# A new table of rank shifts, an earlier first weight chunk, and a last output tile copied out in halves

## The chip, the cores and the metric

The kernel runs on one core of a Trainium2 chip. The metric is device microseconds (us) of one execution, as a median of several runs; lower is better. In the profile PE is TensorE (matmuls), DVE is VectorE, ACT is ScalarE, POOL is GpSimd and SP is SyncE, which here issues the DMAs.

## The reference

Three blocks run one after the other, all in fp32 (B=4, H=8, S=576, D=64; 2304 tokens, d_model 512, d_ff 768 and 2048):

```python
# attention, causal, with a bias from a running sum of s
scores = q @ k.T / sqrt(D)
cum    = cumsum(max(s, 0))
scores = where(causal, -1e9, scores + min(-(cum_i - cum_j), 0))
attn   = softmax(scores)
x      = (attn @ v).reshape(tokens, 512)
# expert block with a maximum
h = max(x @ w1, x @ w2, x @ w3);  x = h @ w_out
# rational block
h = x @ w_in
P = a0 + a1*h + a2*h^2 + a3*h^3;  Q = 1 + |b0|*|h| + |b1|*h^2
out = (P / (Q + 1e-6)) @ w_out2
```

## The kernel before, in words

The 32 heads are worked in 16 pairs, numbered 0 to 15. The work on a pair has these steps, each a function of the kernel:

- load: q and k (raw_k, raw_q) and v come in by DMA; `dm` (L279) is the one line that issues all DMAs, on SP's queue. The first two pairs' q and k are 288 KB each.
- prep and prep_pe: q and k are transposed and split into a high and a low part (L485 on PE, L492, or L500 on DVE), into the tile qkT. The bias rows of the running sum go into the tiles EXT, by DMA out of PT, where the running sum is worked out at the start (L410 to L452).
- scores: PE multiplies qkT and EXT (L548) into PSUM banks; DVE adds the causal mask and takes row maxima (L575, tiles P and PD; the results go to the tile small).
- norm: DVE works out the normalising factors (L601, L602), ACT takes the exponentials, POOL scales P and PD (L592).
- flip: PE turns P and PD by a matmul with an identity (L659, L654), and ACT, DVE or POOL copy the result into PT (L273).
- values: PE multiplies PT with v (L721) into a bank, in two parts per pair: part 0 is 256 columns, part 1 is 320. The high half is copied out by ACT or DVE (L273), and the low half is formed by DVE (L734). The bank is free only after L734.

Every product that needs full fp32 is made of three passes over high and low halves. Of the four pairs of a batch come 288 tokens at a time of x, and the experts (L222, 12 or 9 matmuls of 288 columns for a group) multiply them with w1, w2 and w3, with the maximum on DVE (L855). A weight chunk is loaded raw (raww, 512 KB), decoded by DVE in three instructions which hold one PSUM bank from the first to the third (L763, L766, L768), and then split into high and low (L273, L276). From about 410 us on, only the expert output and the rational block run (L1027 to L1106).

The order of the instructions is not the order of the source. Each function hands steps to a `Plan` (L44): a list of engines that may do it, a rank, what it reads and writes, and how many of the eight PSUM banks it takes and frees. `Plan.issue` (L93) is a list scheduler: it keeps a clock of its own for each engine, takes the step that can start first, and between several ready on one engine takes the one with the lowest rank. A step for which several engines are named is given to one by this same clock. A bank is handed out in the order in which the banks come free by that clock. What comes out is one fixed queue for each engine; on the chip every engine works through its queue in order and waits by semaphores for data and for banks. `MOVES` (L19) is a table that is added to the ranks: a key such as ("values", (2, 1)) shifts the step "values" of pair 2, part 1, by so much.

On SP's queue the first five DMAs are s and the q and k of pairs 0 and 1. Then come the EXT rows (which wait for DVE's L452), and then the rest. A weight chunk's load names the first two EXT DMAs, `e_dma[:2]`, as steps that must be placed ahead of it (`weights`, L806).

The last output block (n = NBLK-1, 384 tokens) has three tiles of 128 rows by 512 columns. After the last matmuls (L1092) tile 0 is copied out of its bank by ACT, tile 1 by DVE, tile 2 by ACT (L1106), and each goes out by a DMA.

Of the kernel before, what the change touches and what calls it, by code (L numbers as in the profile page):

```python
# [16 lines left out]


MOVES = {k: x for kind, moves in {  # L19
    "flip": {(1, 0): 0.65, (1, 3): -1.55, (1, 4): 1.7, (3, 2): 1.05, (3, 3): 1.0, (5, 0): 0.1, (5, 3): -0.15,  # L20
        (8, 0): 0.6, (10, 0): 0.7, (12, 1): 1.35, (13, 0): 1.35, (13, 1): 1.4},
    "load v": {5: -0.35, 6: 0.6},
    "norm": {(4, 1): 0.55, (13, 1): -1.2},
    "prep": {3: 1.0, 4: 1.45, 14: 1.75},
    "regroup": {6: 0.65, 8: 1.15, 9: 1.1, 12: 1.5},
    "scores": {(0, 3): -1.1, (1, 1): 0.3, (1, 3): -0.95, (3, 2): -1.9, (3, 3): -0.4, (4, 0): 0.1, (4, 1): 0.6,
        (4, 2): 0.25, (5, 2): -0.1, (6, 1): -0.55, (7, 0): 0.75, (7, 3): 0.95, (9, 2): 0.55, (10, 3): 0.85,
        (11, 0): 1.1, (13, 3): 1.75, (14, 2): 1.85},
    "spill": {0: 0.7, 3: 1.55, 4: 1.5, 10: 0.6, 14: -1.9, 16: -1.3, 18: -1.1, 20: -1.25},
    "values": {(2, 1): 0.65, 5: 0.6, 6: 1.3, 7: 0.35, 9: 1.05, 10: 2.0, 11: 1.0, 12: 1.65, 13: 2.0, 14: 0.75},  # L30
# [3 lines left out]
}.items() for k, x in ((((kind, *k) if isinstance(k, tuple) else (kind, k)), x) for k, x in moves.items())}  # L34


# [134 lines left out]
def kernel(  # L171
# [20 lines left out]
    nc = tc.nc  # L192
    B, H, S, D = q.shape
    NT, DM = out.shape
# [7 lines left out]
    NBLK = NT // TB  # L202
# [48 lines left out]
    def ve(rank, n, fn, reads=(), writes=(), free=(), cost=None):  # L251
        return plan.add({"dve": cost or c_dve(n)}, rank, fn, reads, writes, (), free)
# [25 lines left out]
    def dm(rank, kb, out, in_, reads=(), writes=(), pre=()):  # L278
        return plan.add({"sp": 0.69 if kb in (64, 80) else 0.5}, rank, lambda: nc.sync.dma_start(  # L279
            out=out() if callable(out) else out, in_=in_() if callable(in_) else in_), reads, writes, kb=kb, pre=pre)  # L280
# [94 lines left out]
        nc.gpsimd.memset(t, 1.0)  # L375
    dm(-9, 74, s_in, s.rearrange("b h s -> (b h) s"), (), ["sc0"])

    def load_qk(pr, rank, pre=()):


        b, h = divmod(2 * pr, H)
        if pr in (0, 1, 2):
            for nm, src in (("k", k), ("q", q)):
                t, key = raw_of(pr, nm)
                dm(rank, 288, t[:, 0:S], src[b, h:h + 2].rearrange("y (p f) d -> (y p) (f d)", p=64),
                   [key], [("raw", pr, nm)], pre)
            return
        for nm, src in (("k", k), ("q", q)):
            t, key = raw_of(pr, nm)
            for y in range(2):  # L390
                x = src[b, h + y].rearrange("(p f) d -> p (f d)", p=32)
                for u in range(2):
                    dm(rank, 143, t[64 * y + 32 * u:64 * y + 32 * u + 32, 0:1120],
                       x[:, 32 * u:32 * u + 1120], [key], [("raw", pr, nm, y, u)], pre)
# [59 lines left out]
    e_dma = []  # L454
# [285 lines left out]
    def cols(w, fc):  # L740

        return w.bitcast(U32).rearrange("(k p) f -> p k f", p=128)[:, :, 256 * fc:256 * fc + 256]
# [4 lines left out]
    def load_raw(rank, dst, src, key, pre=()):  # L747

        def view():
            r = dst() if callable(dst) else dst  # L750
            return r.rearrange("p (k f) t -> p k (f t)", k=src.shape[1]) if len(src.shape) == 3 else r.rearrange("p f t -> p (f t)")

        dm(rank, 512, view, src, (), [key], pre=pre)
# [26 lines left out]
    spill = [x[1:] for x in need if x[1:] not in DIRECT]  # L780
# [25 lines left out]
    def weights():  # L806
        for i in range(3 * KF1):
            fc, m = divmod(i, 3)
            plan.tag = ("w", i)
            rank = m_rank(0, 6 * fc) - 1.6  # L810
            r = raww[i % 2]
            key = w13_key[m, fc] = wkey()

            def new(m=m, fc=fc):
                w13[m, fc] = wslot(f"w13_{fc}_{m}")

            plan.add({"ctl": 0.0}, rank, new, (), [key, "w order"])
            load_raw(rank, r, cols((w1, w2, w3)[m], fc), ("raww", i % 2), e_dma[:2])
            decode(rank, lambda r=r: r, lambda i=i: wx[i % 2], ("raww", i % 2), ("wx", i % 2), True)
            split(rank, lambda i=i: wx[i % 2].bitcast(F32), lambda m=m, fc=fc: w13[m, fc], ("wx", i % 2), key, PR(0 if i < 6 else 9))  # L820
        for i, (kind, x) in enumerate(spill):
            plan.tag = ("spill", i)
            rank = S0 + (S1 - S0) * i / len(spill)
            r = raww[i % 2]
            load_raw(rank - 0.3, r, w2_src(kind, x), ("raww", i % 2))
            decode(rank, lambda r=r: r, lambda i=i: wx[i % 2], ("raww", i % 2), ("wx", i % 2), True)
            dm(rank, 256, w2_dram[i], wx[i % 2].bitcast(F32), [("wx", i % 2)], [("spill", i)])
        plan.tag = None
# [253 lines left out]
    def m2_out(rank, n, fc):  # L1082
        kg = ("g", (n * KF2 + fc) % 4)
        for tt in range(TB // 128):
            if fc == 0:
                acc[n, tt] = Hold()
            hold = acc[n, tt]

            def mms(tt=tt, hold=hold):
                ts = slice(128 * tt, 128 * tt + 128)  # L1090
                for x, (ga, wb) in enumerate(((0, 0), (0, 1), (1, 0))):
                    nc.tensor.matmul(hold.bank, t2[kg][:, ga, ts], w2["o2", fc][:, wb, :],  # L1092
                                     start=(fc == 0 and x == 0), stop=(fc == KF2 - 1 and x == 2))

            pe(rank, 3 * 0.231, mms, [kg, w2_key["o2", fc]], [("acc", n, tt)], take=[hold] if fc == 0 else ())
            if fc == KF2 - 1:
                key, = hkeys(1)
                o = {}

                def new(o=o, tt=tt):  # L1100
                    o[0] = pools["p2"].tile([128, DM], F32, tag="h", bufs=KF1, name=f"o{n}_{tt}")

                plan.add({"ctl": 0.0}, rank, new, ["p2"], [key, "h order"])
                on_v = n == NBLK - 1 and tt == 1
                (ve if on_v else ac)(rank, DM, lambda o=o, hold=hold, on_v=on_v: (
                    nc.vector.tensor_copy(o[0], hold.bank) if on_v else nc.scalar.copy(out=o[0], in_=hold.bank)),  # L1106
                    [("acc", n, tt)], [key], free=[hold])
                r0 = n * TB + 128 * tt
                dm(rank, 256, out[r0:r0 + 128, :], lambda o=o: o[0], [key], [("out", n, tt)])

    for dc in range(KM):
        moe1_out(R0 - 0.5, 0, dc)
# [55 lines left out]
```

## Time and profile before

| | |
|---|---|
| runs shown | 867.02 us median of 3 (866.91 to 868.51) |
| profiled execution | 867.21 us, of which the span is 865.4 |
| PE | busy 855.2 us (99%), 6316 matmuls |
| DVE | busy 678.5 us (78%) |
| ACT | busy 531.9 us (61%) |
| POOL | busy 402.1 us (46%) |
| TensorE clock granted | 1.0 in all of the span |
| HBM | 69.96 MB read, 21.60 MB written, 106 GB/s |

The span is what the profiler saw from the first to the last instruction or transfer; 1.8 us of the execution lie around it. Busy time is the sum over an engine's instructions; an engine that is 99% busy can only become faster by having less work or by losing the 1%. The chain that ended last is 95% PE by the page.

### The profile page before, as it was taken

How to read it: one execution, taken by the hardware profiler on the slowest of the kernel's cores; microseconds unless marked ns; L12 is line 12 of the kernel's file. 1: busy time of each engine (PE TensorE's matmuls, PEld its weight loads, DVE VectorE, ACT ScalarE, POOL GpSimd, SP SyncE). 2: the span in 40 equal slices, each digit the busy share in tenths (PEclk: the TensorE clock that was granted, in tenths of full speed). 3: DMA queues.
4: the chain of work that ended last, by engine and by line, in shares of the span. 5: the costliest groups of instructions: out<-in, count | busy, mean ns of one | idle time of the engine just before them, and what ended most of it. 6: DMA issues, size and time to landing. Idle time of an engine off the chain costs nothing.

```text
span 865.4 us, 17650 instructions
## 1 busy us (share of the span) xinstructions
PE 855.2 (99%) x6316; PEld 797.1 (92%) x6316; DVE 678.5 (78%) x1547; ACT 531.9 (61%) x1193; POOL 402.1 (46%) x549
## 2 busy tenths in 40 slices
PE   8899999999999999999999999999999999999998
PEld 7788999999999999999899999999999999999996
DVE  7999998999998875875993886578568748865785
ACT  6887777766766661226763765476367637654664
POOL 5576786756656440007642543354255325432332
PEclk9999999999999999999999999999999999999999
DMA  5987878878866645853000200020020001000100
GB/s 147 217 211 204 220 188 240 227 221 236 240 191 190 202 165 184 291 146 115 1 1 28 65 1 1 28 65 1 1 74 19 1 28 65 0 2 1 37 1 36
DMA packets 80566, 92.77 MB, mean 107 GB/s; under 512 B 33696, under 2 KB 61856, under 8 KB 80448
## 3 DMA queue, kind: packets, MB, share of 16 engines
q1 hardware_dynamic: 80480, 91.67, 36.8%
q8 instruction: 49, 0.80, 0.4%
q14 instruction: 37, 0.30, 0.1%
HBM read 69.96 MB, written 21.60 MB: 106 GB/s over the span
## 4 chain that ended last, share of the span: by engine, by line
PE 95%; DVE 1%; POOL 1%; DMA 1%; issue 0%; ACT 0%; SPq 0%; POOLq 0%; DVEq 0%
PE bank L222 58%; PE bank L1092 23%; PE bank L548 6%; PE bank L721 5%; PE bank L659 2%; PE bank L654 1%; DMA v<-in_v_dram 0%; DMA EXT<-PT 0%; DVE PD L575 0%; PE bank L485 0%; POOL mask L418 0%; POOL PD L592 0%; POOL qkT L276 0%; ACT PD L583 0%; POOL EXT L413 0%
## 5 line engine op out<-in xcount | busy, mean ns | idle before, releaser
L222 PE MATMUL bank<-x,w 128*128 128x288 f32 x1728 | 238.6, 296 | 0.0
L222 PEld LDWEIGHTS bank<-x,w 128*128 128x128 f32 x1728 | 230.2, 188 | 1.9 <-issue 0.2
L1092 PE MATMUL bank<-ws,g 128*128 128x512 f32 x864 | 215.6, 393 | 0.0
L222 PE MATMUL bank<-x,ws 128*128 128x384 f32 x1008 | 190.2, 336 | 0.0
L1092 PEld LDWEIGHTS bank<-ws,g 128*128 128x128 f32 x864 | 160.9, 188 | 29.5 <-DVE g L1072 0.3
L222 PEld LDWEIGHTS bank<-x,ws 128*128 128x128 f32 x1008 | 178.2, 188 | 7.1
L1048 POOL TENSOR_SCALAR q<-a,cf 128x384 f32<-128x384 f32 x96 | 66.2, 690 | 182.5 <-ACT a L1043 181.3
L1050 POOL TENSOR_TENSOR q<-q,a 128x384 f32<-128x384 f32 x96 | 98.4, 1025 | 8.0
L1065 DVE SCALAR_TENSOR_TENSOR q<-q,cf,bank 128x384 f32<-128x384 f32 x96 | 58.8, 613 | 50.7 <-ACT bank L1063 48.0
L276 POOL TENSOR_TENSOR h<-h 128x384 fp32r<-128x384 f32 x30 | 31.2, 1061 | 136.9 <-ACT h L959 136.9
L1071 ACT CAST g<-t 128x384 fp32r<-128x384 f32 x96 | 49.4, 514 | 49.6 <-DVE t L1069 49.6
L1060 ACT ACTIVATE a<-q,cf 128x384 f32<-128x384 f32 x96 | 59.3, 617 | 31.3 <-POOL q L1050 30.5
L222 PE MATMUL bank<-h,ws 128*128 128x384 f32 x432 | 75.9, 336 | 0.0
L222 PEld LDWEIGHTS bank<-h,ws 128*128 128x128 f32 x432 | 75.0, 188 | 0.5
L1043 ACT ACTIVATE a<-bank 128x384 f32<-128x384 f32 x96 | 47.0, 489 | 41.0 <-PE bank L222 40.5
L1051 DVE TENSOR_TENSOR t<-bank,t 128x384 f32<-128x384 f32 x96 | 52.9, 551 | 21.6 <-ACT t L1045 21.6
L273 POOL COPY PT<-PD 32x576 f32<-32x576 f32 x94 | 62.2, 661 | 14.2 <-DVE PD L634 9.9
L1045 ACT ACTIVATE t<-bank,cf 128x384 f32<-128x384 f32 x96 | 64.0, 666 | 0.0
L1052 DVE SCALAR_TENSOR_TENSOR t<-t,cf,bank 128x384 f32<-128x384 f32 x96 | 58.8, 612 | 2.4
L1069 DVE SCALAR_TENSOR_TENSOR t<-t,cf,bank 128x384 f32<-128x384 f32 x96 | 58.7, 611 | 2.4
L855 DVE TENSOR_TENSOR hs<-bank,hs 128x288 f32<-128x288 f32 x96 | 43.0, 448 | 20.2 <-PE bank L222 19.2
L592 POOL TENSOR_SCALAR PD<-PD,small 128x640 f32<-128x640 f32 (+3 forms) x38 | 27.6, 736 | 63.3 <-DVE small L602 57.6
(115 smaller groups left out, 1370.4 us busy)
## 6 DMA issues: line engine op xcount, KB each, us to landing
raww<-in_moe_w_out_dram SPq DMA_DIRECT2D x22, 512.0 KB, 4.2
raww<-in_moe_w_dram SPq DMA_DIRECT2D x18, 512.0 KB, 4.5
w_dram<-wx SPq DMA_DIRECT2D x36, 256.0 KB, 4.5
ws<-w_dram SPq DMA_DIRECT2D x36, 256.0 KB, 4.5
raw_k<-in_k_dram SPq DMA_DIRECT2D x52, 140.0 KB, 6.4
raw_q<-in_q_dram SPq DMA_DIRECT2D x52, 140.0 KB, 4.3
raww<-in_moe_w_in_dram SPq DMA_DIRECT2D x14, 512.0 KB, 5.2
h_dram<-hs SPq DMA_DIRECT2D x48, 144.0 KB, 3.4
```

What stands on the lines that cost most here:

```text
L222: nc.tensor.matmul(ps, l, r, start=begin and i == 0, stop=end and i == len(seq) - 1)
L273: nc.scalar.copy(out=out, in_=in_) if e == "act" else (nc.vector if e == "dve" else nc.gpsimd).tensor_copy(out, in_)
L548: nc.tensor.matmul(holds[g][y].bank[0:nr, at0:at0 + j1 - j0], l[h, r0:r0 + nr], keys, start=(x == 0), stop=(x == len(ops) - 1))
L1045: ac(rank, 0, lambda: nc.scalar.activation(out=t2[kt], in_=hold.bank[:, 0:TB], func=ACTF.Identity, scale=cf[:, 3:4], bias=cf[:, 2:3]), [(" ...
L1048: po(rank, 0, lambda: nc.gpsimd.tensor_scalar(t2[kq], t2[ka], cf[:, 5:6], cf[:, 4:5], ALU.mult, ALU.add), [ka, "cf4"], [kq], cost=0.75)
L1050: po(rank, 0, lambda: nc.gpsimd.tensor_tensor(t2[kq], t2[kq], t2[ka], ALU.mult), [ka], [kq], cost=0.97)
L1051: ve(rank, TB, lambda: nc.vector.tensor_tensor(t2[kt], hold.bank[:, 0:TB], t2[kt], ALU.mult), [("hp", ci)], [kt])
L1052: ve(rank, 0, lambda: nc.vector.scalar_tensor_tensor(t2[kt], t2[kt], cf[:, 1:2], hold.bank[:, 0:TB], ALU.add, ALU.mult), [("hp", ci), ("h ...
L1060: ac(rank, 0, lambda: nc.scalar.activation(out=t2[a], in_=t2[qq], func=ACTF.Ln, bias=cf[:, 6:7], scale=1.0), [kq, "cf6"], [ka], cost=0.52)
L1065: ve(rank, 0, lambda: nc.vector.scalar_tensor_tensor(t2[qq], t2[qq], cf[:, 6:7], hold.bank[:, 0:TB], ALU.add, ALU.mult), [kr], [kq], cost= ...
L1069: ve(rank, 0, lambda: nc.vector.scalar_tensor_tensor(t2[t], t2[t], cf[:, 0:1], hold.bank[:, 0:TB], ALU.add, ALU.mult), [kr, turn], [kt], f ...
L1092: nc.tensor.matmul(hold.bank, t2[kg][:, ga, ts], w2["o2", fc][:, wb, :], start=(fc == 0 and x == 0), stop=(fc == KF2 - 1 and x == 2))
```

## The change

Four edits. The table of rank shifts has other keys and other values; the load of weight chunk 0 no longer names the EXT DMAs as steps to be placed ahead of it; `load_qk` has got a parameter whose default keeps what it did; and the last output tile is copied out of its bank in two halves, columns 0 to 255 by ACT and 256 to 511 by DVE, with the DMA behind both. The lines of the new file are 1 further down between L378 and L1090 (L548 is L549), and the copies at the end are L1109 and L1112.

```diff
 MOVES = {k: x for kind, moves in {
-    "values": {(2, 1): 0.65, 5: 0.6, 6: 1.3, 7: 0.35, 9: 1.05, 10: 2.0, 11: 1.0, 12: 1.65, 13: 2.0, 14: 0.75},
+    "values": {(2, 1): 1.7, (3, 1): 1.0, 7: 0.95, 8: 1.1, 9: 0.7, 11: 2.0},
...
-    def load_qk(pr, rank, pre=()):
+    def load_qk(pr, rank, pre=(), names="kq"):
...
-            for nm, src in (("k", k), ("q", q)):
+            for nm in names:
+                src = {"k": k, "q": q}[nm]
...
-            load_raw(rank, r, cols((w1, w2, w3)[m], fc), ("raww", i % 2), e_dma[:2])
+            load_raw(rank, r, cols((w1, w2, w3)[m], fc), ("raww", i % 2), e_dma[:2] if i else ())
...
-                (ve if on_v else ac)(rank, DM, lambda o=o, hold=hold, on_v=on_v: (
-                    nc.vector.tensor_copy(o[0], hold.bank) if on_v else nc.scalar.copy(out=o[0], in_=hold.bank)),
+
+                half = DM // 2 if n == NBLK - 1 and tt == 2 else DM
+                (ve if on_v else ac)(rank, half, lambda o=o, hold=hold, on_v=on_v, half=half: (
+                    nc.vector.tensor_copy(o[0], hold.bank) if on_v else nc.scalar.copy(out=o[0][:, 0:half], in_=hold.bank[:, 0:half])),
                     [("acc", n, tt)], [key], free=[hold])
+                if half < DM:
+                    ve(rank, half, lambda o=o, hold=hold, half=half: nc.vector.tensor_copy(o[0][:, half:], hold.bank[:, half:]),
+                       [("acc", n, tt), "h order"], [("o", "end")])
                 r0 = n * TB + 128 * tt
-                dm(rank, 256, out[r0:r0 + 128, :], lambda o=o: o[0], [key], [("out", n, tt)])
+                dm(rank, 256, out[r0:r0 + 128, :], lambda o=o: o[0], [key] + [("o", "end")] * (n == NBLK - 1 and tt == 2), [("out", n, tt)])
```

The number of matmuls is the same. What the edits do to the queues is shown at three places.

The first is the start of the program. SP's queue there, before, from its second DMA on; raww_108 is the buffer of weight chunk 0, and EXT_94 and EXT_95 are the bias rows of pairs 0 and 1.

```order
L279 DMA raw_k<-in_k_dram 128x576
L279 DMA raw_q<-in_q_dram 128x576
L279 DMA raw_k<-in_k_dram 128x576
L279 DMA raw_q<-in_q_dram 128x576
L279 DMA EXT_94<-PT 8x1x1152
L279 DMA EXT_95<-PT 8x1x1152
L279 DMA ext_dram<-PT 32x2880
L279 DMA raw_k<-in_k_dram 128x576
L279 DMA raw_q<-in_q_dram 128x576
```

The same stretch of SP's queue now:

```order
L279 DMA raw_k<-in_k_dram 128x576
L279 DMA raw_q<-in_q_dram 128x576
L279 DMA raw_k<-in_k_dram 128x576
L279 DMA raw_q<-in_q_dram 128x576
L279 DMA raww_108<-in_moe_w_dram 128x4x256
L279 DMA EXT_94<-PT 8x1x1152
L279 DMA EXT_95<-PT 8x1x1152
L279 DMA ext_dram<-PT 32x2880
L279 DMA raw_k<-in_k_dram 128x576
```

The weight chunk, which had been the 24th DMA, stands sixth, in front of the bias rows; pair 2's raw_q has moved behind four loads of v.

The second place is where the values of pair 3 end and the next scores of pair 4 begin. DVE's queue there, before (x3_127 is the x tile that the values fill):

```order
L500 STREAM_TRANSPOSE T_k_93<-raw_k_89 128x18x32
L734 TENSOR_TENSOR x3_127<-bank1_67,x3_127 128x320
L500 STREAM_TRANSPOSE T_q_92<-raw_q_88 128x18x32
L273 COPY PT_100<-bank4_70 128x4x128
L273 COPY PT_100<-bank2_68 128x4x128
```

The same place of DVE's queue now (x3_130 is the x tile of pair 3 there, and raww0_108 is a weight chunk):

```order
L735 TENSOR_TENSOR x2_126<-bank1_67,x2_126 128x256
L764 TENSOR_SCALAR bank3_69<-raww0_108 128x512
L273 CAST x3_130<-bank7_73 128x320
L273 COPY PT_100<-bank0_66 128x3x128
L735 TENSOR_TENSOR x3_130<-bank7_73,x3_130 128x320
L767 SCALAR_TENSOR_TENSOR bank3_69<-raww0_108,bank3_69 128x512
```

The subtraction for pair 3's values of 320 columns frees bank7 now, and bank1 before; it is the 176th entry of DVE's queue, and was the 170th.

PE's queue at the same place, before, from the values of pair 3 to the scores of pair 4 (PD_96 holds scaled scores, qkT0_90 the q and k of pair 4).

```order
L721 MATMUL bank1_67<-PT_100 64x64 x2
L222 MATMUL bank6_72<-x0_124,w13_0_1_129 128x288
...
L659 MATMUL bank7_73<-ident_87,PD_96 128x128 x3
L659 MATMUL bank4_70<-ident_87,PD_96 128x128 x4
L659 MATMUL bank2_68<-ident_87,PD_96 128x128 x4
L222 MATMUL bank5_71<-x3_127,w13_0_0_128 128x288 x3
L222 MATMUL bank6_72<-x3_127,w13_0_1_129 128x288 x3
L548 MATMUL bank1_67<-qkT0_90 128x256
L548 MATMUL bank7_73<-qkT0_90 128x256
```

The same place of PE's queue now:

```order
L722 MATMUL bank7_73<-PT_100 64x64 x2
L660 MATMUL bank0_66<-ident_87,PD_96 128x128 x3
L660 MATMUL bank6_72<-ident_87,PD_96 128x128 x4
L660 MATMUL bank1_67<-ident_87,PD_96 128x128 x4
L549 MATMUL bank0_66<-qkT0_90 64x64
L549 MATMUL bank7_73<-qkT0_90 64x64
```

In both orders the next scores of pair 4 take the bank into which the values of pair 3 went (bank1 before, bank7 now). Before, 15 expert matmuls and the flips stand between the two, now the flips alone.

The third place is the end of the program: the last rows of ACT's queue and then of DVE's, before (o5_0 to o5_2 are the last three output tiles, and what an instruction waits for stands in brackets):

```order
L1071 CAST g2_3_5501<-t2_3_5493 128x384 [waits DVE_49,PE_49]
L1106 COPY o5_0_8826<-bank4_70 128x512 [waits PE_49]
L1106 COPY o5_2_8828<-bank0_66 128x512 [waits PE_49]
L1072 TENSOR_TENSOR g2_3_5501<-t2_3_5493,g2_3_5501 128x384 [waits PE_49,Activation_49]
L1106 COPY o5_1_8827<-bank6_72 128x512 [waits DMAHW4_49,DMAHW3_49,DMAHW5_49,DMAHW2_49,PE_49]
```

The same ends now, ACT's two rows first and then DVE's three:

```order
L1109 COPY o5_0_8826<-bank7_73 128x512 [waits PE_49]
L1109 COPY o5_2_8828<-bank6_72 128x256 [waits DVE_49]
L1073 TENSOR_TENSOR g2_3_5501<-t2_3_5493,g2_3_5501 128x384 [waits PE_49,Activation_49]
L1109 COPY o5_1_8827<-bank3_69 128x512 [waits DMAHW4_49,DMAHW3_49,DMAHW5_49,DMAHW2_49,PE_49]
L1112 COPY o5_2_8828<-bank6_72 128x256 [waits DMAHW7_49,DMAHW6_49,PE_49]
```

ACT's copy of the last tile waits for DVE where it waited for PE; DVE's half stands behind DVE's copy of tile 1.

## Rows read from the trace of the kernel before

**Rows 1.** Busy time by stretch: stretch, length, then busy (instructions) of each engine.
```profile
core 0: us, PE busy (x) PEld busy (x) DVE busy (x) ACT busy (x) POOL busy (x), PEclk, DMA share, GB/s
16.50:73.00 56.50, 53.48 (x606) 45.34 (x602) 55.01 (x174) 47.62 (x145) 32.10 (x46) 1.00 0.84 201
73.00:861.60 788.60, 788.55 (x5475) 739.62 (x5475) 611.96 (x1340) 474.47 (x1026) 360.76 (x478) 1.00 0.33 99
```

**Rows 2.** PE's waits up to 73 us: total us, times, longest.
```profile
PE bank L659 <- POOL PD L592: 1.5, 2, 1.4
PE bank L440 <- POOL ident masks.py:199: 1.5, 1, 1.5
PE bank L485 <- DVE small L575: 1.5, 1, 1.5
PE bank L721 <- ACT PT L273: 0.6, 1, 0.6
PE bank L721 <- DVE PT L273: 0.6, 1, 0.6
PE bank L548 <- DMA EXT<-PT: 0.4, 1, 0.4
```

**Rows 3.** Busy time by stretch, DVE alone.
```profile
0.00:58.30 58.30, 51.95 (x171) 1.00 0.79 193
```

**Rows 4.** DVE's timeline to 16.5 us: start, length, instruction, [idle before it <- releaser].
```profile
11.05 0.49 DVE L575 CUSTOM_DVE_ANT_0 P<-bank,mask 128x320 f32<-128x320 f32 x1 [0.62 <-PE bank L548]
...
16.50 0.62 DVE L575 CUSTOM_DVE_ANT_0 PD<-bank,mask 128x448 f32<-128x448 f32 x1 [1.19 <-PE bank L548]
```

**Rows 5.** DVE's groups, 16.5 to 73 us: count, busy us, mean ns, idle before.
```profile
L763 DVE TENSOR_SCALAR bank<-raww 128x512 uint32<-128x512 uint32 x6 | 4.1, 676 | 0.0
L734 DVE TENSOR_TENSOR x<-bank,x 128x256 fp32r<-128x256 f32 x4 | 1.6, 410 | 0.0
L273 DVE CAST x<-bank 128x320 fp32r<-128x320 f32 x1 | 0.5, 450 | 0.0
```

**Rows 6.** DVE's timeline at the values of pair 3.
```profile
57.82 0.48 DVE L734 TENSOR_TENSOR x<-bank,x 128x320 fp32r<-128x320 f32 x1
58.22 1.23 DVE L500 STREAM_TRANSPOSE T_q<-raw_q 128x576 f32<-128x576 f32 x1
59.30 1.26 DVE L273 COPY PT<-bank 128x512 f32<-128x512 f32 x2
60.49 0.20 DVE L575 CUSTOM_DVE_ANT_0 P<-bank,mask 64x64 f32<-64x64 f32 x1
```

**Rows 7.** PE's timeline at the scores of pair 4.
```profile
57.30 1.42 PE L659 MATMUL bank<-ident,PD 128*128 128x128 f32 x11
58.47 1.04 PE L222 MATMUL bank<-x,w 128*128 128x288 f32 x6
59.44 0.62 PE L548 MATMUL bank<-qkT 64*128 64x256 f32 x6
```

**Rows 8.** The chain that ended last: start, length, piece, matmuls in it.
```profile
155.75 1.78 PE bank L222 x12
...
158.07 1.58 PE bank L222 x12
```

**Rows 9.** SP's timeline, two DMA issues of the first 7 us.
```profile
2.60 0.43 SPq L279 DMA_DIRECT2D raw_q<-in_q_dram  x1
6.72 1.54 SPq L279 DMA_DIRECT2D EXT<-PT  x2
```

**Rows 10.** The chain's piece for the bias rows.
```profile
6.72 3.23 DMA EXT<-PT
```

**Rows 11.** DMA busy by stretch, last two columns: share, GB/s.
```profile
4.00:5.00 1.00, 1.00 (x14) 0.78 (x15) 1.00 (x1) 0.00 (x0) 1.00 (x1) 1.00 1.00 339
6.00:7.00 1.00, 1.00 (x42) 1.00 (x40) 0.94 (x2) 0.59 (x1) 1.00 (x2) 1.00 0.05 18
```

**Rows 12.** Timeline of the end, ACT and DVE.
```profile
860.91 0.69 DVE L1106 COPY o<-bank 128x512 f32<-128x512 f32 x1 [2.86 <-PE bank L1092]
861.59 0.59 ACT L1106 COPY o<-bank 128x512 f32<-128x512 f32 x1 [0.77 <-PE bank L1092]
```

**Rows 13.** ACT's groups over the whole program.
```profile
L273 ACT CAST x<-bank 128x256 fp32r<-128x256 f32 x16 | 5.9, 366 | 2.8 <-PE bank L721 2.8
```

More of the change, by code (lines that the diff above doesn't have):

```diff
@@ L19 @@
 MOVES = {k: x for kind, moves in {
[L20 to L29, printed above, removed]
-    "values": {(2, 1): 0.65, 5: 0.6, 6: 1.3, 7: 0.35, 9: 1.05, 10: 2.0, 11: 1.0, 12: 1.65, 13: 2.0, 14: 0.75},
[3 rows of a table removed]
+    "flip": {(2, 2): 0.15, (2, 3): 0.45, (3, 3): -0.2, (3, 4): -1.15, (5, 0): -1.3, (11, 0): -1.1, (12, 1): 1.95,
+        (14, 0): 0.8},
+    "load v": {2: 0.55, 12: -0.2, 13: 0.25},
+    "norm": {(0, 1): 1.55, (2, 1): -0.45, (14, 1): 0.1, (14, 3): 1.75, (15, 3): 2.0},
+    "prep": {2: 1.6, 3: 0.8},
+    "regroup": {8: 1.8, 9: 1.95, 10: 0.55, 12: 1.6},
+    "scores": {(1, 1): 1.55, (1, 3): -1.45, (4, 0): -0.7, (5, 0): 0.55, (6, 2): 0.8, (7, 1): 1.9, (7, 2): -1.4,
+        (8, 0): -0.9, (9, 1): -0.35, (10, 2): -1.25, (10, 3): -0.55, (12, 1): 1.45, (12, 3): 1.9, (13, 3): -1.15,
+        (14, 1): -1.9, (15, 2): -1.15, (15, 3): 0.7},
+    "spill": {0: 1.95, 1: 1.75, 2: 0.75, 4: 0.55, 6: -1.35, 10: -1.2, 11: -0.25, 14: -1.8, 25: 1.7, 27: -1.1},
+    "values": {(2, 1): 1.7, (3, 1): 1.0, 7: 0.95, 8: 1.1, 9: 0.7, 11: 2.0},
[3 rows of a table added]
 }.items() for k, x in ((((kind, *k) if isinstance(k, tuple) else (kind, k)), x) for k, x in moves.items())}
```

6 rows, old and new, of the table MOVES are left out of this document.

## The prediction

> **What bounds the kernel now.** I read the busy time by stretch first, then PE's waits, then DVE's queue, then the end. From 73 us to the last matmuls PE is busy for 788.55 of 788.60 us [rows 1]: nothing waits there, so a moved instruction can gain nothing there, and costs something only if it makes PE wait. Between 16.5 and 73 us PE lacks 56.50 - 53.48 = 3.02 us, and DVE only 56.50 - 55.01 = 1.49. There DVE is nearly as full as PE, and the two bound the start together. All of PE's waits of more than 0.3 us in the first 73 us are six groups, 6.1 us in all [rows 2]: the first identity (1.5), the bias rows (0.4), a raw_k of pair 2 charged to DVE (1.5, at 12.6 us), and flips and values that wait for P, PD and PT behind DVE, ACT and POOL (2.7). What the change is worth is therefore decided in the first 73 us, in how PE passes between kinds of matmul, and in the copies behind the last matmul. The sum is made against the profiled execution, 867.21 us; the median of the runs shown lies 0.19 below it. By less than 0.2% of it (1.7 us) a measurement of this kernel can't tell a change from none: "same" is 865.3 to 868.75.
>
> **The queues of the first 60 us.** The table moves DVE's work, it hardly removes any. The point to watch is the subtraction that ends pair 3's 320-column values and frees their bank: the next scores of pair 4 take that bank in both orders. Before, it ended at 58.29 (57.82 + 0.48, less rounding) [rows 6], and the scores began at 59.44 [rows 7], so the bank had been free for 1.15 us and PE didn't wait for it. Now I set DVE's work in front of it against that of before. Successive starts give the net prices: a copy of a flipped block 0.59 (two from 59.30 to 60.49), a transpose 1.08 (58.22 to 59.30) [rows 6]; by the same overlap of about 0.08 to a mean, a decode step 0.59 and a high half 0.35 to 0.45 [rows 5].
> No longer in front of it: one high half of q and k (0.68), three flips (0.60, 0.47, 0.47), two weight splits (0.35, 0.41), a decode step (0.59): 3.6 us. New in front of it: five flips and one decode step (6 x 0.59 = 3.5), a weight subtraction (0.60), three high halves of values that were ACT's (3 x 0.45 = 1.35), a q transpose of pair 5 (1.08): 6.6 us. That is +3.0 us of DVE's work ahead of the same instruction.
> Against it: chunk 0 is loaded early, so DVE can decode it in holes in which it stood before. These are 0.62 us at 11 and 1.19 at 16.5 [rows 4]; two decode steps, 1.2 us, fill them. The instruction then ends at 58.3 + 3.0 - 1.2 = 60.1 us.
> PE meanwhile has less in front of those scores: fifteen expert matmuls have gone from the place between values and scores, others have come ahead; counted by durations, it has 1.9 us less to do there, which is 59.44 - 1.94 = 57.5 with the waits it had before. It would stand from 57.5 to 60.1 and some 0.05 for the signal: 2.65 us. What PE lost by a late DVE afterwards, about 0.6 us near 68 and 72, goes, since DVE's work after this point is the less. Net: **+2.0 us**. Nothing later gives it back, for after 73 us PE has no idle time out of which to take it [rows 1].
> The bounds. Upward: if ACT's queue, which also has more in front of pair 2's and 3's values, makes DVE wait, I get +3.0. Downward: DVE has to do 55.2 us of work by that point, and before it had stood 58.30 - 51.95 = 6.35 us by then [rows 3]; of that at least 2.9 are the beginning, when its inputs have not arrived. So it can't be done before 58.1: PE waits 0.6 there, and the 0.6 saved later pays for it: 0.
>
> **The early chunk.** It is issued behind the fourth load of q and k (from 2.60) instead of behind the EXT rows (from 6.72) [rows 9], at about 3.1, and moves 512 KB in front of them. At the 339 GB/s of the first loads that is 512 KB / 339 = 1.5 us; from 6 to 7 us the DMA engines are at 0.05 of their capacity [rows 11]. By that the first loads are done at about 6, so the chunk ends near 7.5, while the EXT rows are issued at 6.72 and landed at 9.95 [rows 10], and their packets start about 8. Cost: between 0 (the hole hides it) and 1.5 (the EXT rows stand behind all of it, and PE's 0.4 on them grows by that). I take 0. No gain by itself: the first experts aren't what PE waits for [rows 2].
>
> **PE's passages.** Twelve expert matmuls behind flips take 1.58, the same twelve behind scores 1.78 [rows 8]: 0.20 for each return from scores or values to the full array. By the two PE queues there were 36 such returns, and there are now 32: 4 x 0.20 = -0.8. Passages between scores and values go from 23 to 23, with the transposes from 29 to 30: +0.1. Together **-0.7 us**, between -1.0 and -0.4 as other neighbours cost a little more or less.
>
> **The last tile.** ACT's copy of the last bank took 0.59 and began with PE's last matmul [rows 12]; DVE was free by then (860.91 + 0.69 = 861.60). Now ACT's half waits for DVE and no longer for PE, and DVE's half waits for PE: the two halves stand one behind the other. 256 columns out of a bank take DVE 0.41 [rows 5] and ACT 0.37 [rows 13]. One behind the other, with some 0.05 between: 0.83 against 0.59, **+0.25 us**. Side by side it would be the longer half, 0.41: -0.2. The Trainium skill, "PSUM — Partial Sum Buffer", in its table of terms under PSUM bank, says that two engines must not access the same bank in the same quadrant at once, reads against reads included; by that rule halves of columns can't be read side by side, and the dependence in the queue is the rule put into practice. No row here shows two engines on a bank at once, and the sum by the rule is the +0.25 that I take from the queue and these rows anyway; without it the term would be -0.2.
>
> The changed `load_qk` issues what it did: 0. POOL's queue has no term of its own: it is busy 32.10 of 56.50 us in the dense stretch [rows 1], and scaled tiles that come late are inside the bounds above.
>
> **Sum:** 867.21 + 2.0 - 0.7 + 0.25 = 868.76; at the median, 0.19 less: 868.6 us.
>
> **The rivals.**
> (a) DVE is relieved: the early decodes free it for the tiles that PE waits for. For it: 2.7 us of PE's waits end on DVE, ACT or POOL behind DVE [rows 2], and 1.2 us of decoding move into its holes. Against it: the +3.0 us in the queue. It holds if the bank for pair 4's scores is free when PE comes. If 1.2 us of those waits and the 0.6 near 70 us go, with -0.7 and +0.25: 867.02 - 2.25 = 864.8, faster.
> (b) The EXT rows stand behind the chunk: one queue of transfers, 512 KB, 1.5 us. PE's first scores come 1.5 later, DVE's masks with them, and as DVE is full until 73 us all of it stays: 868.6 + 1.5 = 870.1, slower. It decides if the chunk's last packet lands after about 8 us. The empty hole at 6 us speaks against it; that the four loads before it keep all DMA engines full at 4 us [rows 11], so that a little delay pushes it into the EXT rows, for it. ACT's bound of +3.0 without any EXT delay gives 869.6, which I count with this case.
> (c) The waits only change their places: the bank is free 0.6 after PE comes, as by the lower bound. 867.02 + 0 - 0.7 + 0.25 = 866.6, same.
>
> **How the numbers follow.** My forecast gets 0.42, its own range 867.9 to 869.4: it straddles the edge of 868.75, and I split it 0.25 same, 0.17 slower. (a) gets 0.22, all faster. (b) gets 0.20, slower. (c) gets 0.16, same. So faster 0.22, same 0.41, slower 0.37. The range takes in (c), (b) and some of (a): 864.9 to 870.8.
>
> **What would show it.** In the changed kernel's profile: PE's waits have one of 2 to 3 us that ends at about 60 us, at L549 on the bank that DVE's L735 frees, and L735 for the 320 columns ends there, not at 58.3; the waits near 68 and 72 us are gone; after 80 us PE still has none. Twelve expert matmuls still take 1.58 or 1.78. At the end ACT's L1109 of 256 columns starts when DVE's L1112 ends, and the last copy ends some 0.8 after the last matmul. The chunk lands before 8 us, and the wait for EXT stays at 0.4. The forecast is wrong if PE's longest wait up to 73 us lies elsewhere, if DVE frees that bank by 58 us, or if PE's idle time grows after 80 us.

## The result, and the profile after

The changed kernel takes 872.64 us (median of 6, 871.49 to 873.38) against 867.70 (median of 6): ratio 1.0051, 95% interval 1.0041 to 1.0062. It is slower by half a per cent, where 868.6 was forecast with "same" as the likeliest outcome, and it lies above the stated range, whose upper end is 870.8. Four of the six runs had a mean granted TensorE clock of 0.996 to 0.998 and took 872.6 to 873.4. The two at 1.00 took 871.5, which is above the range as well, and most runs of before at 1.00 took 866.8 to 868.5, so some 4 us of the 5 are the change at an even clock. The profiled execution is one of these two, 871.49 us, with a span of 869.9 against 865.4.

Busy time by stretch, after; the columns are those of [rows 1]:

```profile
16.50:73.00 56.50, 51.84 (x595) 43.05 (x594) 55.30 (x175) 48.06 (x144) 34.15 (x48) 1.00 0.83 194
73.00:90.00 17.00, 16.13 (x163) 14.41 (x163) 16.66 (x44) 11.98 (x36) 9.86 (x13) 1.00 0.76 206
90.00:865.90 775.90, 775.60 (x5326) 727.93 (x5324) 598.33 (x1301) 463.02 (x990) 346.55 (x459) 1.00 0.31 96
```

PE lacks 4.66 us from 16.5 to 73 us where it lacked 3.02, then 0.87 more up to 90 and 0.3 after that. PE's waits in the changed kernel, whole program, to be read against [rows 2]:

```profile
PE bank L722 <- ACT PT L273: 1.5, 2, 1.1
PE bank L441 <- POOL ident masks.py:199: 1.5, 1, 1.5
PE bank L486 <- DMA raw_k<-in_k_dram: 1.4, 1, 1.4
PE bank L549 <- DMA EXT<-ext_dram: 1.4, 1, 1.4
PE bank L660 <- DVE x L735: 0.5, 1, 0.5
PE bank L222 <- DVE wx L769: 0.5, 1, 0.5
PE bank L660 <- DVE PT L273: 0.5, 1, 0.5
PE bank L660 <- DVE small L576: 0.4, 1, 0.4
PE bank L549 <- DVE PT L273: 0.2, 1, 0.2
PE bank L222 <- DVE hs L856: 0.2, 1, 0.2
PE bank L549 <- DVE x L735: 0.2, 1, 0.2
```

Seven kinds of waits (those of [rows 2] and one of 0.3) have become eleven. PE's idle time over the whole span grew by only 2.5 us (10.2 to 12.7 us). Its busy time grew by 2.0 with the same 6316 matmuls. Much of that is the first matmul behind a wait, which has a longer record (0.41 us for the two EXT matmuls behind the wait at 28 us, 0.31 elsewhere), so that such a wait costs more than its row says. Counted from the start of one matmul to the start of the next, over what the same pair of matmuls takes elsewhere, the last matmul begins 4.39 us later, and that is made of:

| | before | after | |
|---|---|---|---|
| waits up to 16.5 us | 2.2 | 1.6 | -0.6 |
| the first 136 transposes | 4.65 | 5.37 | +0.7 |
| waits from 16.5 to 62 us | 2.8 | 6.3 | +3.5 |
| waits from 62 to 90 us | 0.7 | 1.1 | +0.4 |
| waits behind 90 us | 0 | 0.7 | +0.7 |
| PE's passages between kinds of matmul | | | -0.9 |
| the rest, differences under 0.06 each | | | +0.6 |

The copies behind the last matmul add 0.23.

The growth of 3.5 us up to 62 us isn't spread evenly. Before, PE's longest wait there was for POOL's PD; in the changed kernel a wait of the same length for pair 2's bias rows stands in its place. Before, then the changed kernel:

```profile
32.54 1.09 PE L659 MATMUL bank<-ident,PD 128*128 128x128 f32 x8 [1.36 <-POOL PD L592]
```

```profile
29.59 0.41 PE L549 MATMUL bank<-EXT 64*128 64x320 f32 x2 [1.37 <-DMA EXT<-ext_dram]
```

Up to 46 us the two kernels differ by 0.6 us. The other 2.9 us lie between 46 and 62 us, where PE waited for nothing before; the first of these waits is 0.53 us, at 47.49 us, for DVE's L735.

### The profile page after: what moved, and what is told of

It reads as the page before. It is cut to its first block, busy times and chain, and to the rows that moved or that the text cites. A ratio compares the mean times of both kernels' runs of the same rounds, so it can differ in the third digit from the quotient of the medians.

```text
span 869.9 us, 17667 instructions
## 1 busy us (share of the span) xinstructions
PE 857.2 (99%) x6316; PEld 798.1 (92%) x6316; DVE 683.3 (79%) x1554; ACT 532.4 (61%) x1192; POOL 399.6 (46%) x544
## 4 chain that ended last, share of the span: by engine, by line
PE 90%; DVE 5%; DMA 3%; issue 1%; POOL 1%; SPq 1%; ACT 0%; POOLq 0%; DVEq 0%; ACTq 0%
PE bank L222 56%; PE bank L1093 23%; PE bank L549 5%; PE bank L722 4%; PE bank L660 1%; DMA raw_k<-in_k_dram 1%; DMA raww<-in_moe_w_dram 1%; SPq L279 1%; DVE PD L576 1%; PE bank L655 1%; DMA ws<-w_dram 1%; DVE bank L764 1%; DVE bank L767 0%; DVE P L576 0%; DVE T_q L501 0%
## 5 line engine op out<-in xcount | busy, mean ns | idle before, releaser
L584 ACT ACTIVATE PD<-PD,small 128x640 f32<-128x640 f32 (+3 forms) x64 | 47.8, 749 | 21.1 <-DVE small L576 19.5
```

## The experiments

A part undone through the source lets the planner write a wholly new order. So two kinds of kernels were run: some with one part of the source alone, and some in which the planner's order was written down first and one or a few steps were moved in it, all else staying where it was. In the diffs, `move(a, b)` puts step a in front of step b of that order, `after(a, b)` behind it. Times "at full clock" are those of runs with a mean granted clock of 0.999 or 1.00.

**The parts alone.** The table without the early chunk, and with the last tile copied whole (`e_moves`; the diff is against the kernel before):

```diff
 MOVES = {k: x for kind, moves in {
-    "values": {(2, 1): 0.65, 5: 0.6, ...
+    "values": {(2, 1): 1.7, (3, 1): 1.0, ...
```

> The kernel before with the new table of rank shifts alone; the first weight chunk behind the bias rows and the last tile copied whole, as before. The planner writes a third order, in which pair 2's bias rows again stand late on SP's queue, behind the coefficients. If the table by itself makes the start dense, PE's waits up to 90 us grow by 2 us or more over before (5.7), and the time is 869.5 to 872 against 868. If the loss comes from the early chunk's place in the queues, the table alone gives the time of before or, by the fewer passages of PE, 0.5 less: 867 to 868.

Measured: 887.19 us, ratio 1.0228 (1.0204 to 1.0252), more than three times the loss of all parts together. Its waits behind 90 us, where before has none and the changed kernel 0.2:

```profile
PE bank L721 <- POOL PT L273: 2.3, 1, 2.3
PE bank L222 <- ACT PT L273: 1.9, 2, 1.1
PE bank L659 <- POOL P L592: 1.3, 1, 1.3
PE bank L654 <- DVE hs L855: 1.0, 2, 0.7
...
```

The early chunk with the old table (`e_early`):

```diff
-            load_raw(rank, r, cols((w1, w2, w3)[m], fc), ("raww", i % 2), e_dma[:2])
+            load_raw(rank, r, cols((w1, w2, w3)[m], fc), ("raww", i % 2), e_dma[:2] if i else ())
```

> The kernel before with the first weight chunk allowed in front of the bias rows, and nothing else; the planner writes a fourth order. If the early chunk's place in the queues makes the loss, the time is 870 to 872; if the table makes it, 867 to 869.

Measured: 874.99 us, ratio 1.0078 (1.0059 to 1.0096). Either part alone has a higher median than both together (for the early chunk the two intervals just touch), so their losses can't be added: each makes the planner write another order. That a table of shifts suits only the order that it was made for fits this, but these two runs don't show more.

**The early transfer by itself** (`x_chunk`: the order of before, with this one DMA moved):

```diff
+    move(96, 16)      # load of weight chunk 0, in front of the first bias rows
```

> The kernel before with one DMA moved: weight chunk 0 is loaded in front of the first bias rows, as in the changed kernel; its decoding and everything else stay where they were. If the chunk only shares the DMA engines with the q and k of pairs 0 and 1 (as in the changed kernel, where the first 136 transposes took 5.4 us for 4.6), the transposes take 0.7 us longer, PE's wait for the first bias rows (0.6) goes, and the time is that of before, 867.7 within 0.3. By case (b) of the prediction the bias rows stand behind the chunk and the time grows by 1 to 1.5 us, 868.7 to 869.2.

Measured: 867.70 us, ratio 0.9996 (0.9987 to 1.0006). PE waits 0.2 and 0.4 us for raw_k and raw_q within the first transposes, and no longer for the bias rows. The transfer by itself costs nothing that this shows (at most 0.5 us by the interval); the loss comes with the order that is written around it.

**The late bias rows of pair 2** (`x_ext`: the order of the changed kernel with one DMA moved). In the changed kernel PE waits 1.4 us at 28 us for this load, issued at 24.3 us where it was issued at 19.3:

```diff
+    move(484, 547)    # EXT<-ext_dram of pair 2, in front of pair 3's raw_k
```

> The changed kernel with one DMA moved: the load of pair 2's bias rows (EXT from ext_dram) goes up SP's queue from behind pair 3's raw_q and the coefficients to in front of pair 3's raw_k, about where the kernel before has it. Nothing else moves on any engine. Theory D (DVE's queue sets the pace from about 49 to 78 us, so a wait that PE loses earlier comes back later): PE's wait of 1.4 us for EXT at 28 us goes, PE's waits from 33 to 78 us grow by as much, and the time falls by 0 to 0.4 us, 872.2 to 872.6, ratio to before 1.005 or a little more. Rival E (the late bias rows are a cause of their own): the 1.5 us are gained in full, about 871.1, ratio 1.004.

Measured: 873.69 us, ratio 1.0050 (1.0036 to 1.0064); 871.1 in the one run at full clock, against 871.5, so of the 1.5 us no more than some 0.4 are gained. One run says little here: some runs of before at that clock took 869 us or more. PE's waits from 25 us on begin with:

```profile
PE bank L660 <- ACT P L591: 1.8, 1, 1.8
PE bank L722 <- ACT PT L273: 1.5, 2, 1.1
```

The wait for EXT is gone, and PE waits 1.8 us for the first flips behind it. This profile alone doesn't tell why: its clock had fallen before (last section), and in `l_after` and `y_pk` below, whose clock fell too, the wait for EXT is gone and the same 1.8 and 1.7 us stand in front of the flips though the load is where it was. That what PE lost at 28 us it would else have lost at 31 fits the time at full clock, but is argued.

**DVE relieved** (`x_dve2`, and `x_extdve2` with the DMA moved too):

```diff
+    for x in seq:     # x[0]: step, x[1]: engine
+        if x[0] in (458, 460, 529, 542, 545, 619, 614): x[1] = "act"
+        if x[0] in (108, 129, 136): x[1] = "pool"
```

> The changed kernel with ten steps of the first 75 us taken from DVE and given to other engines at the same places of the order: four flip copies and three high halves of values to ACT (about 3.6 us of DVE's work), three weight subtractions to POOL (about 1.8 us). Theory D: PE's waits between 46 and 78 us, now 4.1 us, shrink by 2 to 3.5 us, and the time falls to 869.1 to 870.6, ratio to before 1.0016 to 1.0034. Rival E: these waits follow from the late bias rows and from DMAs, and the time stays at 872.6, ratio 1.0057. A third case: ACT, busy 40 of 45 us there, becomes what PE waits for, and the time stays or grows; then the waits carry ACT's name.

> Both edits of the two kernels before this one: the earlier load of pair 2's bias rows, and the ten steps taken from DVE. Theory D: once DVE is relieved the wait at 28 us counts as well, so it gains 0.5 to 1.5 us over the kernel with the ten steps alone: 868 to 870. Rival E: 871.1, as with the bias rows alone.

Measured: 872.08 us, ratio 1.0047 (1.0033 to 1.0062), and 873.28, ratio 1.0049 (1.0037 to 1.0062); at full clock 871.4 to 872.1 and 872.0. Theory D's gain isn't there. PE's waits from 30 to 80 us in `x_dve2`:

```profile
PE bank L722 <- ACT PT L273: 2.0, 2, 1.1
PE bank L549 <- DMA EXT<-ext_dram: 1.8, 1, 1.8
PE bank L660 <- ACT PT L273: 0.5, 1, 0.5
PE bank L549 <- ACT PT L273: 0.4, 1, 0.4
...
```

Apart from EXT, which grew by 0.4, and two of 0.2 that aren't shown here, they carry ACT's name now, the third case: work taken off DVE is work on ACT, which holds the next step.

**Less work for DVE and none more for others** (`l_before`, `l_after`: the orders of before and of the changed kernel; of the three decoding instructions the middle one is left out for each of the first eight weight chunks, so that the weights lack bits):

```diff
+    seq[:] = [x for x in seq if x[0] not in range(98, 98 + 7 * 8, 7)]
```

> The kernel before in its own order, with one of the three decoding instructions left out on DVE for each of the first eight weight chunks (the middle one, so the weights lack bits): about 8 x 0.6 = 4.8 us of DVE's work less, most of it before 85 us, and nothing more for any other engine. By the theory that DVE is the second bound of the start, some of PE's 2.8 us of waits from 30 to 43 us and 0.7 us from 67 to 73 go: 0.5 to 2 us faster than before, 866 to 867.5. By the rival that PE's waits there are the delay of a chain from engine to engine, nothing: 868.

> The changed kernel in its own order, with the same eight instructions left out. By the theory that DVE's load is what the new order runs into, its 4.1 us of waits from 46 to 78 us fall to 1 or less, and it comes within 1 us of the other kernel without these instructions: 867 to 869. By the rival that in the new order PE reaches steps just after the steps that they depend on, so that it waits for the way PE to ACT or DVE and back however free these are, 2.5 us or more of the waits stay: 870 to 871.5.

Measured: 867.50 us, ratio 0.9985 (0.9974 to 0.9996), and 871.78, ratio 1.0037 (1.0023 to 1.0050); at full clock 865.9 to 867.1, and 871.0 in the one such run. The old order gains about a microsecond; the new one gains half of one, though two of its waits behind 73 us are gone. The wait of 1.1 us for PT stays:

```profile
PE bank L660 <- ACT P L591: 1.8, 1, 1.8
PE bank L722 <- ACT PT L273: 1.5, 2, 1.1
PE bank L549 <- DVE PT L273: 0.6, 1, 0.6
PE bank L549 <- DVE x L735: 0.2, 1, 0.2
```

**The order around the wait of 1.1 us.** In the changed kernel PE does pair 3's first flips at 55.06 us and has nothing else between them and the values that need them; ACT copies the flips only at 56.27, behind two exponentials:

```profile
55.06 0.63 PE L660 MATMUL bank<-ident,P 128*128 128x128 f32 x4
55.53 0.54 PE L655 MATMUL bank<-ident,P 128*128 128x128 f32 x3
55.90 0.38 PE L660 MATMUL bank<-ident,P 128*128 128x128 f32 x2
57.38 0.34 PE L722 MATMUL bank<-PT 128*64 128x64 f32 x4 [1.09 <-ACT PT L273]
```

```profile
54.95 0.67 ACT L584 ACTIVATE PD<-PD,small 128x448 f32<-128x448 f32 x1 [0.71 <-DVE small L576]
...
55.62 0.65 ACT L584 ACTIVATE PD<-PD,small 128x448 f32<-128x448 f32 x1
...
56.27 1.05 ACT L273 COPY PT<-bank 128x512 f32<-128x512 f32 x3
```

Before, 32 matmuls of pair 4's scores stood between flips and values. In the changed kernel 16 of them stand in front of the flips and 16 behind the values. `y_swap` moves the first 16 back between the two (its expectation speaks of 32), `y_swap_light` with the eight instructions left out as well:

```diff
+    after(730, 607)   # scores of pair 4, behind the flips of pair 3
```

> The changed kernel with one step of PE's queue moved: the 32 matmuls of pair 4's first scores go from in front of pair 3's first flips to behind them, so that they stand between these flips and pair 3's first values, as in the kernel before. Theory L (order and distance: in the new order the values stand directly behind the flips they need, so PE waits for the way over ACT, 1.2 us at 56 us, whatever the engines' load): the wait of 1.2 us in front of the values goes. But the flips' own inputs are ready only at about 55 us, so that PE may wait up to 1 us in front of the flips instead: 870.3 to 871.5 at full clock against 871.5. By theory D nothing changes, since DVE's queue decides when pair 3's scores are scaled: 871.5.

> The same move, and the eight decoding instructions left out as in the kernel with less work for DVE. Theory L: with DVE lighter the flips' inputs are ready earlier, and the 1.2 us which that kernel still lost in front of the values go: 1 to 1.3 us faster than it, about 869.8 to 870 at full clock. If the wait comes back elsewhere: 871.

Measured: 872.95, ratio 1.0051 (1.0038 to 1.0064), at full clock 872.2 or more; and 872.57, ratio 1.0052 (1.0040 to 1.0064). In `y_swap` the wait moved: 1.1 us in front of the flips, charged to DVE's small, and nothing was gained. The flips' inputs were late too. With 16 matmuls of the 32, this isn't a full test of the old place of these scores. `y_pk` takes one step out of the way of the masks that make them, `y_pk_light` with less work besides:

```diff
+    after(794, 583)   # transpose of pair 5's k, behind the masks and factors of pair 3
+    after(862, 794); after(863, 862)   # the two loads into its buffer follow it
```

> The changed kernel with one step of DVE's queue moved: the transpose of pair 5's k (1.1 us, whose data land at 49.0 us) goes from in front of the four masks of pair 3's second scores to behind them and the factors made of them (the two loads that reuse its buffer follow it). Theory H (head of the queue: the masks stand behind a transpose that waits for its transfer, the scaling stands behind the masks, the flips behind the scaling, the values behind the flips): the masks come 1.1 us earlier, PE's waits from 54 to 57 us, now 1.4, fall by 0.5 to 1.1 us, and the time at full clock falls to 870.4 to 871.0. Theory D (only DVE's total work counts): the same work stands in front of pair 4's scores, so PE waits there instead: 871.5.

> The same move in the kernel without the eight decoding instructions. There DVE stood idle in front of that transpose until the transfer landed, so that the lighter queue gained nothing before 57 us. Theory H: now the lighter queue counts, PE's waits between 54 and 62 us, 2.2 in that kernel, fall to 1 or less, and the time at full clock falls from 871 to about 869.7. If they stay, the transfer is not what held the lighter queue.

Measured: 872.54, ratio 1.0049 (1.0033 to 1.0065), at full clock 871.4 and 872.6: nothing. And 870.55, ratio 1.0031 (1.0020 to 1.0043), at full clock 869.6 to 869.9 with one run of 870.6: some 1.2 us under the kernel with the lighter DVE alone, as theory H has it, though the wait of 1.1 us itself stays. That kernel has one run at full clock (871.0), and the intervals of the two ratios overlap, so this step isn't clear of noise. Both moves together:

> The changed kernel with both moves: pair 5's k transposed behind the masks of pair 3's second scores, and pair 4's first scores behind pair 3's first flips. Either alone left 1.2 us of waiting in front of the values or of the flips. If the two waits are one chain (late masks, late flips, then values directly behind them), both moves together break it: PE's waits between 54 and 58 us fall from 1.4 to 0.5 or less and the time at full clock to 870.3 to 870.8 against 871.5. If not, a wait of about 1.2 us stays at one of the two places: 871.4 or more.

> The same two moves without the eight decoding instructions, where the first move alone gave 869.7 at full clock. If order and load together make the waits, this one falls by another 0.7 to 1.2 us, to 868.5 to 869, within 1 to 2.5 us of the old order without these instructions (866.5 at full clock). If the wait only moves, 869.7.

Measured: 873.34, ratio 1.0054 (1.0041 to 1.0067), and 871.75, ratio 1.0035 (1.0021 to 1.0049). The chain isn't broken: in `y_pk_swap` PE waits 1.0 us in front of the flips, now under POOL's name. POOL's scaling of P stands there behind a copy and two subtractions; the profile ends the wait at POOL's next copy, so which of them held PE isn't settled.

**What the early slot is worth.** PE's wait at 12.6 us, in [rows 2] under DVE's name, is for pair 2's raw_k. `z_rawk` gives the slot in front of the bias rows to it, `z_rawkq` to pair 2's q too (order of before), `a_rawkq` does the same in the order of the changed kernel and puts the chunk behind the bias rows:

```diff
+    move(20, 16)      # raw_k of pair 2, in front of the first bias rows
+    move(21, 16)      # raw_q of pair 2 (not in z_rawk)
+    after(96, 22)     # a_rawkq only: weight chunk 0 behind the bias rows
```

> The kernel before with one DMA moved: pair 2's k is loaded in front of the first bias rows, into the slot that the change gave to the weight chunk. It lands near 8 us, long before PE asks for it at 12.6. If the raw_k of pair 2 is what PE waits for there (1.6 us, charged to DVE by the waits), the wait falls to what raw_q of pair 2 and DVE leave of it, and up to 1.6 us are gained: 866 to 867. If DVE sets the pace, PE's gain comes back as a wait near 15 or 31 us: 867.5. Where the granted clock falls behind this wait in some runs (times of 869 instead of 867.5), it stays at 1.00 in all.

> The same with pair 2's q in front of the bias rows too. Both are there when PE asks for them at 12.6 us, but 576 KB take 1.7 us of the DMA engines behind the first loads, to about 7.7 us, and the bias rows begin at 8. If the bias rows aren't delayed: 865.9 to 867 and the granted clock 1.00 in all runs. If they are, PE waits for them near 10 us, up to 1 us longer, and half of the gain is gone.

> The changed kernel with the early slot given to pair 2's k and q, and the weight chunk loaded behind the bias rows. In the kernel before, the same slot for k and q gained about 1.3 us at full clock. If that wait of 1.6 us at 12.6 counts in the new order as well: 870 to 870.5 at full clock, and the granted clock stays at 1.00 in nearly all runs. If the new order's later waits set the pace: 871.5, with the waits behind 28 us longer by as much.

Measured: `z_rawk` 868.67 us, ratio 0.9999 (0.9989 to 1.0008), with 866.0 to 869.9 in single runs; `z_rawkq` 866.78, ratio 0.9982 (0.9972 to 0.9991); `a_rawkq` 877.45, ratio 1.0106 (1.0090 to 1.0123). In `z_rawkq` the matmuls that began at 14.31 begin at 12.80:

```profile
12.59 0.28 PE L548 MATMUL bank<-EXT 64*128 64x256 f32 x2
12.80 1.15 PE L485 MATMUL bank<-ident,raw_k 64*64 64x64 f32 x32
```

Up to 73 us the later waits keep their length and come 1.2 us earlier: DVE, 98% busy there, wasn't the limit. In this profiled run (866.80) part of the gain is lost again by a new wait of 0.5 us for ACT's x behind 200 us; in that of `z_rawk` (865.99) nothing is. In the other runs of `z_rawk` something else must be late: eight of twelve took more than 868 us, some of them at full clock. In `a_rawkq` DVE, then PE, show why the new order can't do without the early chunk:

```profile
16.26 0.69 DVE L764 TENSOR_SCALAR bank<-raww 128x512 uint32<-128x512 uint32 x1 [6.01 <-DMA raww<-in_moe_w_dram]
```

```profile
PE bank L549 <- DVE qkT L493: 5.0, 1, 5.0
```

The first decoding step stands tenth among DVE's instructions, in front of the last high and low parts of q and k; when its chunk is late, everything behind it is.

**A version below both** (`z_best`): `z_rawkq`, with POOL's scaling of pair 1's PD in front of a copy and a subtraction:

```diff
+    after(557, 456); after(559, 557)
```

> The kernel before with pair 2's k and q in front of the bias rows and, on POOL, the scaling of pair 1's PD tiles (1.4 us) moved in front of the 1.4 us subtraction and the copy for pair 3's q and k, behind which PE waited for it at 31 us. If nothing else holds the flips there, PE's wait of 1.4 us goes: 1.0 to 1.4 us under the kernel with k and q alone, 864.5 to 865.5 at full clock and below both kernels. If the subtraction that is now later holds the scores of pair 3 at 35 us, the wait moves there: 866.

Measured: 866.14 us, ratio 0.9980 (0.9968 to 0.9992), no clear step beyond `z_rawkq`: POOL now stands idle 1.87 us for ACT's PT in front of that scaling, and PE's wait there is 1.0 us instead of 1.3.

## Why the prediction was wrong

- **DVE's queue at pair 4's scores: right in place and time.** L735 for 320 columns was to end at 60.1 us; it ended at 60.69. DVE had done 55.55 us of work by then (the prediction counted 55.2; its rows give 51.95 + 3.0 = 54.95), and had stood 5.14 us instead of 6.35, the 1.2 us less that were forecast. Its start, and DVE's work up to its end (stretch, length, DVE busy with its instructions, granted clock, DMA share, GB/s):

```profile
60.21 0.48 DVE L735 TENSOR_TENSOR x<-bank,x 128x320 fp32r<-128x320 f32 x1
```

```profile
0.00:60.69 60.69, 55.55 (x177) 1.00 0.80 189
```

- **The first step that failed: "It would stand from 57.5 to 60.1".** PE was to reach this bank at 57.5 and wait 2.65 us there. It came at 60.10 (58.68 + 1.42) and waited 0.25 us for a PT in front of the first of these scores, and 0.16 for the bank itself:

```profile
58.68 1.42 PE L660 MATMUL bank<-ident,PD 128*128 128x128 f32 x11
60.35 0.24 PE L549 MATMUL bank<-qkT 64*64 64x64 f32 x1 [0.25 <-DVE PT L273]
60.74 0.36 PE L549 MATMUL bank<-qkT 64*64 64x64 f32 x5 [0.16 <-DVE x L735]
```

The 57.5 was reckoned "with the waits it had before", and PE had lost more by then: 3.5 us more than before by 62 us, in the 1.4 for EXT at 28 us and in waits of 0.2 to 1.2 us from 31 us on. That 3.5 is near the 2.65 is luck: no one wait of that length exists, and the prediction's own sign of being wrong, PE's longest wait lying elsewhere, came true. The sum over DVE's queue told how late that point would be; it didn't tell that PE would be late by itself. In a sum over queues a copy on ACT that is issued long before counts as done; how far behind its matmul it stands, and what is in front of it on ACT, does not enter. That is how the wait of 1.1 us for PT was missed.
- **The second is the next one: "What PE lost by a late DVE afterwards, about 0.6 us near 68 and 72, goes", and nothing costs anything behind 73 us.** The waits behind 62 us grew from 0.7 to 1.8 instead of going. This is 1.7 us of the 2.7 by which the profiled execution (871.49) lies above the sum that was made for it (868.76); the first step (3.5 for 2.65) is 0.9, and the smaller differences nearly cancel. By [rows 1] the old order has no wait there; that the new one would have none was taken over from it, and these runs show an order with 9.0 us of such waits (`e_moves`).
- **Without a term: the granted clock.** The median lies another 1.2 us above the profiled execution, among the four runs with a lower mean clock, for which the sum had nothing.
- **The early chunk at 0: right in sum (+0.1), by another way.** Neither the hole nor case (b) came about: it shared the DMA engines with the first q and k, the transposes took 0.7 longer, and the wait for the bias rows, 0.6, went.
- **PE's passages, -0.7: right**, -0.9. Twelve expert matmuls still take 1.58 or 1.78, thirty-six 4.77 or 5.00.
- **The last tile, +0.25: right**, 0.23, in the durations that were forecast. ACT's half begins 0.03 us after DVE's has ended:

```profile
865.30 0.69 DVE L1109 COPY o<-bank 128x512 f32<-128x512 f32 x1 [2.88 <-PE bank L1093]
865.98 0.42 DVE L1112 COPY o<-bank 128x256 f32<-128x256 f32 x1
866.43 0.37 ACT L1109 COPY o<-bank 128x256 f32<-128x256 f32 x1 [1.23 <-DVE o L1112]
```

The order agrees with the Trainium skill's rule ("PSUM — Partial Sum Buffer", table of terms, PSUM bank) that two engines must not access one bank in one quadrant at once; no run here lets the two read side by side.
- **Not looked at:** pair 2's bias rows, moved behind pair 3's q on SP. Its wait of 1.4 us is the changed kernel's longest of a new kind; the one run of `x_ext` at full clock puts its cost at some 0.4.

What stays open is one cause for the 3.5 us before 62 us. DVE's load alone is not it, nor the late bias rows, nor the k of pair 5, nor the place of 16 of pair 4's scores: each was moved, none gained as much as a microsecond, and where waits went others came in the chain from masks over scaling and flips to values. Only less work on DVE together with the k moved gained more (871.5 to 869.7 at full clock), and about one microsecond of that is what less work gains in the old order too. The loss from 46 us on has no parallel in the old order, so that is where to look next. That the new order sets the steps of a pair closer together on several queues at once fits this, but is argued, not shown.

## What to carry to other kernels

Where several engines are nearly full and the queues are fixed, a queue's sum tells when a point is reached, and not what each wait is worth: follow each dependent pair of steps over all the engines between them, and ask what stands ahead of it on each. A new order is a new kernel: that the old one had no waits in a stretch says nothing of the new one, and parts of a change that share a planner can't be priced by taking one out. A free slot early in the DMA queue is best tried on the load that an engine is seen to wait for, as long as no order has been built on what stands in it (`a_rawkq`), and a wait that carries another engine's name may be that load.

## What the hardware showed that was not expected

The granted TensorE clock fell after a long wait. In `x_ext` PE waited about 2 us from 12.6 us on; the stretch behind it ran at 0.50, the lower of the two levels (1.2 GHz), and so did part of the stretch from 30 us (stretch, length, PE busy, granted clock, DMA share, GB/s):

```profile
0.00:12.60 12.60, 10.19 (x196) 1.00 0.69 198
12.60:14.70 2.10, 0.25 (x6) 1.00 0.52 123
14.70:18.00 3.30, 3.25 (x40) 0.50 0.81 200
18.00:22.00 4.00, 4.00 (x57) 0.99 0.54 131
...
30.00:40.00 10.00, 8.20 (x77) 0.83 0.86 199
```

In the profile of before PE waited 1.5 us at the same place and kept 1.00. The wait's length alone doesn't decide: in their profiles `y_pk` waited 1.4 us there and then ran at 0.50, while `y_swap` waited 1.7 us and kept 1.00. So a run can lose more than the wait itself: of the runs of before some took 867, others 869 to 870, most of these at a mean clock of 0.996 to 0.998. In `z_best`, where pair 2's k and q come early, ten of twelve runs took 865.9 to 866.9; in `z_rawk`, with k alone early, eight of twelve still took more than 868. Some of those eight had a mean clock of 0.999 or 1.00, so the clock isn't all that makes a run slow, and what else does is open.
